# One kernel of attention, routed experts and a two-layer net: bias rows in another PSUM pool, added matmuls, earlier loads, other engines for two copies

## The chip, the core and the metric

The kernel runs on one core of a Trainium2 chip. The core has five engines with a queue each: TensorE (PE, its weight loads PEld), VectorE (DVE), ScalarE (ACT), GpSimd (POOL) and SyncE (SP), which here issues nearly all DMAs. The metric is the device time of one execution in microseconds. Comparisons are between medians of runs.

## What is computed

Three blocks follow each other: attention with a bias that depends on positions, a mixture of eight experts with one expert for each token, and a two-layer net with a cosine.

```python
# q, k, v: 4 batches x 8 heads x 576 x 64
scores = q @ k.T / 8
x = log1p(abs(i - j)) / log1p(max(i, 1))            # 576 x 576
bias = relu(x * w1 + b1) @ w2                       # 32 hidden units, one column for each head
attn = softmax(scores + bias) @ v
x = attn, heads side by side                        # 2304 tokens x 512
e = argmax(x @ w_gate)
x = gate(x) * sigmoid(x @ w_output_gate) * (relu(x @ w1[e]) @ w2[e])
h = x @ w_in                                        # 2304 x 2048
out = (h * cos(h)) @ w_out                          # 2304 x 512
```

All products are made in full fp32 precision: each factor is split into a high and a low part, and three products of parts are added.

## The kernel before

**The bias rows** (`bias_table`). The 576 rows of the bias are made in 36 groups of 16, in the order of `ROWS`. For a group, VectorE and ScalarE make four hidden tiles (hhD, hhA), TensorE multiplies them by w2 into a PSUM tile of two banks (`ps`, three of them in a pool that lives for this stage alone), ScalarE copies that into an SBUF tile `ev` (five buffers), and SP writes it to the DRAM tensor Bd. After the copy of a group, `after` (L480 on) issues loads that read bias rows back, by the table `BIAS_LOAD`: the entry for each of five blocks of query rows is the place in `ROWS` behind which its loads are put. `after` also makes the splits of the first pair, and at the last two groups it loads the q and k (Rqk), the V and the gating table of what comes next. `first` loads the first pair at the start.

**Attention.** The 16 pairs (two heads, one batch) are walked through in five steps u each. In a step, TensorE makes the scores of two query tiles into `ps_s` (two PSUM tiles of two banks, each step uses both), VectorE adds the bias rows (Bp, Bq), takes the minimum mn and leaves s, ScalarE takes the exponentials e, TensorE transposes the e of the step before into Tp (pool `ps_t`, two banks), ScalarE and VectorE copy that to eT, and TensorE multiplies eT by V into pa. The V products of a pair's second half run in the first steps of the next pair. `split` makes high and low parts (HL) of the next pair's q and k on GpSimd. Every engine's queue is in order, and the code's order is the queue's.

**The two-layer net** (`moe2`). The 2304 tokens are six groups of 384. A unit is a group with one half of the hidden units, eight steps of 128; the first six units are half 0 of each group, the next six are half 1. In step s TensorE makes the first layer's tile ph of step s (12 matmuls of 384 columns) and the second layer's part of step s - 4 (9 matmuls of 512 columns, into three PSUM tiles py). Between them stand tk (ScalarE, L1313), three instructions of VectorE that reduce the argument (L1318 to L1320), sine and square (ScalarE), tg (VectorE, L1403), gh (ScalarE, L1409) and gl (GpSimd, L1410). Meanwhile VectorE converts weights from 64-bit to 32-bit numbers (f32a, raw, L701 to L710). At the end of a unit of half 0 the three py are copied to SBUF (o) with factor -2 and written to Y1: the first and third by ScalarE (L1438), the second by VectorE (L1440). The next group's tokens are loaded to xg (one buffer) and split into xh (`split_x`, ScalarE) and xl (`lower_x`, GpSimd), one of four parts in each of steps 1 to 4 and 2 to 5 of a unit. The load of the group after that is issued in a unit's last step.

Of the kernel before, what the change touches and what calls it, by code (L numbers as in the profile page):

```python
# [331 lines left out]
BIAS_ON = _share()  # L332


def bias_table(tc, h, Bd, first, after):


    nc = tc.nc
    NQ = S // 4
    with tc.tile_pool(name="p0", bufs=1) as c, \  # L340
         tc.tile_pool(name="p0h", bufs=10) as hp_, \
         tc.tile_pool(name="p0e", bufs=5) as ep, \
         tc.tile_pool(name="p0ps", bufs=3, space=PSUM) as pp:
        W = c.tile([128, S], F32, name="W")
        cc = c.tile([128, 34 + NQ + S // 16], F32, name="cc")
        near, far = slice(0, 336), slice(336, S)
        nc.sync.dma_start(out=W[:, near], in_=h["t_rel"][:, near])
        nc.scalar.dma_start(out=cc, in_=h["cc"])
        nc.sync.dma_start(out=W[:, far], in_=h["t_rel"][:, far])
        first()  # L350
        w1c, b1c, w2b, psi, rp8 = cc[:, 0:1], cc[:, 1:2], cc[:, 2:34], cc[:, 34:34 + NQ], cc[:, 34 + NQ:]
        bp = c.tile([128, NQ], F32, name="bp")
        nc.vector.tensor_scalar(out=bp, in0=psi, scalar1=b1c, scalar2=None, op0=ALU.mult)
        slope = lambda t: nc.vector.tensor_scalar(out=W[:, t], in0=W[:, t], scalar1=w1c, scalar2=None, op0=ALU.mult)
        slope(near)
        pss = {}

        def evac(G):
            back, ahead = reach(G)
            ev = ep.tile([128, S + 15], F32, name="ev")  # L360
            ps, zero = pss.pop(G)
            parts = [(ev[:, 0:back + ahead], ps[:, zero - back:zero + ahead])]
            if G in MIRROR:
                parts = [(ev[:, 0:back], ps[:, 1:back + 1][:, ::-1]), (ev[:, back:back + ahead], ps[:, 0:ahead])]
            for dst, src in parts:
                nc.scalar.activation(out=dst, in_=src, func=AF.Copy, scale=rp8[:, G:G + 1])
            nc.sync.dma_start(out=Bd[:, 16 * G:16 * G + 16, S - 1 - back:S - 1 + ahead].rearrange("h i j -> i h j"),
                              in_=ev[:, 0:back + ahead])
            after(G)

        for at, G in enumerate(ROWS):
            ps = pp.tile([128, 1024], F32, name="ps")
            back, ahead = reach(G)
            n = max(back + 1, ahead)
            hs = []
            for ct in range(4):
                m = 4 * G + ct
                e = BIAS_ON[m]
                hh = hp_.tile([128, S], F32, name="hh" + e, bufs=dict(D=11, A=5)[e])
                hs.append(hh)  # L380
                if e == "A":
                    nc.scalar.activation(out=hh[:, 0:n], in_=W[:, 0:n], func=AF.Relu, bias=bp[:, m:m + 1], scale=1.0)
                else:
                    nc.vector.tensor_scalar(out=hh[:, 0:n], in0=W[:, 0:n], scalar1=bp[:, m:m + 1], scalar2=0.0,
                                            op0=ALU.add, op1=ALU.max)
            zero = 512 if max(back, ahead) <= 512 else back
            cuts = sorted({zero - back, zero, 512, zero + ahead})
            if G in MIRROR:
                zero, cuts = 0, [0, n]
            pss[G] = ps, zero  # L390
            for c0, c1 in zip(cuts, cuts[1:]):
                for ct in range(4):
                    x = hs[ct][:, c0 - zero:c1 - zero] if c0 >= zero else hs[ct][:, zero - c1 + 1:zero - c0 + 1][:, ::-1]
                    nc.tensor.matmul(ps[32 * ct:32 * ct + 32, c0:c1], w2b, x, start=True, stop=True)
            if at == 2:
                slope(far)
            if at >= 2:
                evac(ROWS[at - 2])
        evac(ROWS[-2])
        evac(ROWS[-1])  # L400


def attention(tc, h, ident, dram, xT, bpool, ps_t, gate, later, dense):
# [3 lines left out]
    with ExitStack() as ctx:  # L407
# [70 lines left out]
        def after(G):  # L478
            at = ROWS.index(G)
            for qt, when in enumerate(BIAS_LOAD):  # L480
                if at == when:
                    for i in range(NTL):
                        if TILES[i][0] == qt:
                            load_bias(0, i)
            if at == len(ROWS) - 3:
                for step in (0, 2, 1, 3):
                    split(0, step, nc.vector)
                split(0, 4)
            if at == len(ROWS) - 2:
                load(1)  # L490
            if at == len(ROWS) - 1:
                load_v(1)
                gate.fetch()

        def first():
            load(0)
            load_v(0)

        bias_table(tc, h, Bd, first, after)
        sp, ep = pool("p1s", 3, **rw), pool("p1e", 1, **rw)  # L500
        ps_s, ps_a = pool("ps_s", 2, space=PSUM, **rw), pool("ps_a", 1, space=PSUM)
        gate.pa = [ps_a.tile([128, 512], F32, name=f"pa{g}") for g in range(2)]
        ET = []
        for g in range(2):
# [3 lines left out]
        def scores(n, u):  # L508

            d = st[n]  # L510
            HL = d["HL"]
            ps = [ps_s.tile([128, 2, 512], F32, name="ps_s") for _ in of_unit(u)]
            for hf in range(2):
                sl = slice(hf * HF, (hf + 1) * HF)
                for x, (q, k) in enumerate(((0, 0), (1, 0), (0, 1))):
                    for par, p in enumerate(ps):
# [4 lines left out]
                            w, y = d["QR"][:, q, :], HL[:, 1, k, sl]  # L521
                        nc.tensor.matmul(p[:, hf, :HF], w, y, start=(x == 0), stop=(x == 2))  # L522
            d["ps"] = ps

        def softmax(n, u):
            d = st[n]
# [137 lines left out]
        gate.pa = None  # L664


BIAS_LOAD = (27, 31, 35, 35, 35)
BIAS_AT = (1, 2, 4)
AV_AT = {1: ((0, 0, 2), (0, 1, 2), (0, 2, 3), (0, 3, 3)),
         4: ((0, 4, 1), (1, 0, 1), (1, 1, 1), (1, 2, 2), (1, 3, 2), (1, 4, 2))}  # L670
# [661 lines left out]
def moe2(tc, h, dram, dense, later, wi, wo, bias, cv):  # L1332
# [4 lines left out]
    with ExitStack() as ctx:  # L1337
# [29 lines left out]
        def split_x(g, c):  # L1367
            if c == 0:
                xsp[g] = dense.x_tiles()
            nc.scalar.activation(out=xsp[g][0][:, c, :], in_=xg[g][:, c, :], func=AF.Copy)  # L1370
# [52 lines left out]
        def layer2(s):  # L1423
# [6 lines left out]
            for t in range(GT // 128):  # L1430
# [3 lines left out]
                if j == HC - 1:  # L1434
                    o = op.tile([128, DM], F32, name="o")
                    if half == 0:
                        if t % 2 == 0:
                            nc.scalar.activation(out=o, in_=acc[t], func=AF.Copy, scale=-2.0)  # L1438
                        else:
                            nc.vector.tensor_scalar(out=o, in0=acc[t], scalar1=-2.0, scalar2=None, op0=ALU.mult)  # L1440
                        nc.sync.dma_start(out=dram["Y1"][rows(g, t), :], in_=o)
                        continue
                    final = s == len(units) * HC - 1 and t == GT // 128 - 1
# [15 lines left out]
        for s in range(N + LAG3):  # L1459
# [11 lines left out]
            if s < N:  # L1471
                k, j = divmod(s, HC)
                if s == 0:
                    load_x(groups[1])
                nx = groups[k + 1]
                if nx != groups[k]:
                    if 1 <= j < 5:
                        split_x(nx, j - 1)
                    if 2 <= j < 6:
                        lower_x(nx, j - 2)  # L1480
                if j == HC - 1 and groups[k + 2] != groups[k + 1]:
                    load_x(groups[k + 2])
            if 0 <= s - LAG3 < N:
# [2 lines left out]
                    load_y(g)  # L1486


CONVERT2_AT = 4
MAGIC = 12582912.0  # L1490
INV2PI = 0.15915494309189535
PI2A = 6.28125
# [59 lines left out]
```

## Time and profile before

| | |
|---|---|
| median of 3 runs | 962.22 us (959.72 to 963.46) |
| the profiled execution | 960.94 us, its span 959.1 us |
| TensorE busy | 917.5 us (96%), weight loads 782.3 us |
| VectorE busy | 712.0 us (74%) |
| ScalarE busy | 549.9 us (57%) |
| GpSimd busy | 305.7 us (32%) |
| mean granted TensorE clock | 0.983 of 2.4 GHz |

The stages, in us from the start of the span: bias rows to about 47, attention to about 300, experts to about 535, the two-layer net to the end. The shares are means over all of them. The granted clock is 1.0 (2.4 GHz) or 0.5 (1.2 GHz) in any stretch, and the mean tells how much of the span lay at the lower level. A busy TensorE is one with matmuls under way; at the lower level each of them takes longer, so its busy share doesn't tell its pace.

### The profile page before, as it was taken

Reading aid. Unit: us, or ns where it says so; the run is one execution under the profiler, and the core shown is the slowest. Engines: PE = TensorE matmul, PEld = TensorE weight load, DVE = VectorE, ACT = ScalarE, POOL = GpSimd, SP = SyncE. Lnnn points to the kernel's source line nnn. Section 1 sums busy time; section 2 is a strip of 40 time slices with the busy share of each in tenths; the row PEclk is TensorE's granted clock in tenths of the full one; section 3 lists DMA queues with packets and bytes.
Section 4 is the critical chain, followed back from the end, with each engine's and each line's share of the span. In section 5 each row is a group of like instructions: output and inputs, shape, how many; then the busy total and the mean of one; then the engine's idle time right before and its main releaser. Section 6 shows DMA issues by size and latency. Waiting matters only on the chain.

```text
span 959.1 us, 19242 instructions
## 1 busy us (share of the span) xinstructions
PE 917.5 (96%) x7145; PEld 782.3 (82%) x7146; DVE 712.0 (74%) x1538; ACT 549.9 (57%) x1157; POOL 305.7 (32%) x394
## 2 busy tenths in 40 slices
PE   7989999999998999999899899999999999999996
PEld 4576666666666999999799789888888899999995
DVE  8956666667777577877795699999999966655652
ACT  8967777777776343353344555555555655555442
POOL 0034344444444022213330044334332433433421
PEclk9979999999999999999999999999999999999999
DMA  7973333523445665548774323443333413211121
GB/s 220 286 249 103 102 134 108 175 65 104 144 155 184 194 204 172 164 122 253 247 243 164 115 83 105 132 143 105 123 102 121 130 58 99 99 53 47 66 67 37
DMA packets 70066, 131.42 MB, mean 137 GB/s; under 512 B 7320, under 2 KB 24748, under 8 KB 69964
## 3 DMA queue, kind: packets, MB, share of 16 engines
q1 hardware_dynamic: 69532, 129.82, 42.2%
q8 instruction: 58, 0.95, 0.4%
q14 instruction: 44, 0.36, 0.1%
q10 hardware_dynamic: 432, 0.29, 0.1%
HBM read 91.76 MB, written 38.32 MB: 136 GB/s over the span
## 4 chain that ended last, share of the span: by engine, by line
PE 51%; DVE 17%; issue 5%; DMA 3%; ACT 1%; SPq 0%; POOL 0%; DVEq 0%; POOLq 0%; ACTq 0%
PE py L1433 12%; PE ph L1384 11%; PE pl L844 9%; PE po L862 8%; PE pa L600 4%; PE ps_s L522 3%; DVE tr L1319 2%; DVE tg L1403 2%; DVE tr L1320 2%; DVE f32a L701 2%; PE Tp L558 2%; DVE raw L708 1%; DVE f32a L703 1%; DVE raw L706 1%; DVE tk L1318 1%
## 5 line engine op out<-in xcount | busy, mean ns | idle before, releaser
L1410 POOL TENSOR_TENSOR gl<-tg,gh 128x384 fp32r<-128x384 f32 x96 | 98.6, 1027 | 253.7 <-ACT gh L1409 179.1
L532 DVE CUSTOM_DVE_ANT_0 s<-ps_s,Bp 128x576 f32<-128x576 f32 x112 | 81.0, 756 | 70.0 <-PE ps_s L522 58.4
L1384 PE MATMUL ph<-xh,w0h 128*128 128x384 f32 x384 | 130.4, 339 | 0.0
L1384 PE MATMUL ph<-xh,w0l 128*128 128x384 f32 x384 | 130.3, 339 | 0.0
L1384 PE MATMUL ph<-xl,w0h 128*128 128x384 f32 x384 | 130.1, 339 | 0.0
L1433 PE MATMUL py<-w1h,gh 128*128 128x512 f32 x288 | 114.7, 398 | 8.1 <-ACT gh L1409 4.5
L1433 PE MATMUL py<-w1h,gl 128*128 128x512 f32 x288 | 114.4, 397 | 0.0
L1433 PE MATMUL py<-w1l,gh 128*128 128x512 f32 x288 | 113.9, 395 | 0.0
L543 ACT ACTIVATE e<-s,mn 128x576 f32<-128x576 f32 x144 | 110.0, 766 | 3.6 <-DVE mn L532 2.6
L1313 ACT ACTIVATE tk<-ph,magic 128x384 f32<-128x384 f32 x96 | 55.1, 574 | 79.3 <-PE ph L1384 78.8
L1320 DVE SCALAR_TENSOR_TENSOR tr<-tk,tr 128x384 f32<-128x384 f32 x96 | 89.6, 933 | 3.3
L1318 DVE TENSOR_SCALAR tk<-tk 128x384 f32<-128x384 f32 x96 | 37.3, 389 | 63.4 <-ACT tk L1313 63.3
L847 ACT ACTIVATE hh<-pl 128x288 fp32r<-128x288 f32 x64 | 26.3, 410 | 100.7 <-PE pl L844 88.1
L522 PEld LDWEIGHTS ps_s<-HL 64*128 64x128 f32 x768 | 58.0, 191 | 30.2 <-DVE eT L571 12.3
L1409 ACT ACTIVATE gh<-tg 128x384 fp32r<-128x384 f32 x96 | 49.7, 518 | 54.3 <-DVE tg L1403 54.0
L844 PE MATMUL pl<-xh,w0h 128*128 128x288 f32 x256 | 78.3, 306 | 2.5 <-DVE hl L848 2.5
L522 PE MATMUL ps_s<-HL 64*128 64x288 f32 x768 | 77.2, 319 | 3.1 <-DVE mn L532 2.3
L844 PE MATMUL pl<-xl,w0h 128*128 128x288 f32 x256 | 76.3, 299 | 2.3 <-DVE xl L816 2.3
L1384 PEld LDWEIGHTS ph<-xh,w0h 128*128 128x128 f32 x384 | 72.8, 190 | 4.0
L1384 PEld LDWEIGHTS ph<-xl,w0h 128*128 128x128 f32 x384 | 72.5, 189 | 3.9
L844 PE MATMUL pl<-xh,w0l 128*128 128x288 f32 x256 | 75.6, 296 | 0.0
L862 PE MATMUL po<-hh,w1h 128*128 128x288 f32 x256 | 75.6, 295 | 0.0
(228 smaller groups left out, 2282.2 us busy)
## 6 DMA issues: line engine op xcount, KB each, us to landing
Bp<-in_w SPq DMA_DIRECT2D x38, 512.0 KB, 5.2
Bd<-ev SPq DMA_DIRECT2D x36, 295.5 KB, 3.8
Rqk<-in_qk SPq DMA_DIRECT2D x16, 576.0 KB, 4.0
raw<-in_w_in SPq DMA_DIRECT2D x32, 256.0 KB, 3.2
raw<-in_w_out SPq DMA_DIRECT2D x32, 256.0 KB, 3.2
Bp<-Bd SPq DMA_DIRECT2D x28, 288.0 KB, 4.3
X<-xT SPq DMA_DIRECT2D x7, 1152.0 KB, 5.1
xg<-X SPq DMA_DIRECT2D x10, 768.0 KB, 5.2
```

What stands on the lines that cost most here:

```text
L522: nc.tensor.matmul(p[:, hf, :HF], w, y, start=(x == 0), stop=(x == 2))
L532: nc.vector.tensor_tensor_reduce(out=h2(s), in0=ps[:, :, :HF], in1=h2(bias(hp, i)), scale=-0.125, scalar=3e38, op0=ALU.add, op1=ALU.min, a ...
L543: nc.scalar.activation(out=e[:, par, :], in_=s, func=AF.Exp, bias=mn, scale=-1.0, accum_out=acc)
L844: nc.tensor.matmul(ps[:, :HF], w[:, c, :], x[:, c, :], start=(n == 0), stop=(n == len(terms) - 1))
L862: nc.tensor.matmul(self.acc[d][:, :HF], w[:, ds_], x, start=(f == 0 and n == 0), stop=(f == self.FC - 1 and n == 2))
L1313: nc.scalar.activation(out=k, in_=hh, func=AF.Identity, scale=INV2PI, bias=magic)
L1318: nc.vector.tensor_scalar(out=k, in0=k, scalar1=-MAGIC, scalar2=None, op0=ALU.add)
L1320: nc.vector.scalar_tensor_tensor(out=r, in0=k, scalar=-PI2B, in1=r, op0=ALU.mult, op1=ALU.add)
L1384: nc.tensor.matmul(ps[:, :GT], w[:, c, :], x[:, c, :], start=(n == 0), stop=(n == 3 * NP_ - 1))
L1409: nc.scalar.activation(out=hi, in_=g, func=AF.Copy)
L1410: nc.gpsimd.tensor_tensor(out=lo, in0=g, in1=hi.bitcast(F32), op=ALU.subtract)
L1433: nc.tensor.matmul(acc[t], x[:, ts_], w, start=(j == 0 and n == 0), stop=(j == HC - 1 and n == 2))
```

## The change

- The PSUM tiles of the bias rows come from attention's own pool `ps_s` (two of each three groups) and from a pool `ps_b` with one tile (the third). `ps_a`, which took banks of its own, takes those of `ps_b` when the bias rows are done. `ev` has eight buffers in place of five.
- All loads of the first two pairs and of the gating table are issued by `first`, at the kernel's start. `BIAS_LOAD` puts the loads of the first three blocks of bias rows behind groups 25, 29 and 32 in place of 27, 31 and 35.
- In the first three steps of the first pair, `FILL` adds 12, 6 and 4 matmuls into the PSUM tiles Tp, whose results nobody reads.
- The three copies o at the end of a unit of half 0 are all ScalarE's.
- In the first unit alone, the next group is split in steps 3 to 6 (high) and 4 to 7 (low); in the others in the steps as before.

```diff
@@ bias_table(tc, h, Bd, bank, first, after)
-         tc.tile_pool(name="p0e", bufs=5) as ep, \
-         tc.tile_pool(name="p0ps", bufs=3, space=PSUM) as pp:
+         tc.tile_pool(name="p0e", bufs=8) as ep:
...
         for at, G in enumerate(ROWS):
-            ps = pp.tile([128, 1024], F32, name="ps")
+            ps = bank(at)
@@ attention, after
                 split(0, 4)
-            if at == len(ROWS) - 2:
-                load(1)
-            if at == len(ROWS) - 1:
-                load_v(1)
-                gate.fetch()
 
         def first():
-            load(0)
-            load_v(0)
-
-        bias_table(tc, h, Bd, first, after)
+            for n in range(2):
+                load(n)
+                load_v(n)
+            gate.fetch()
+
+        ps_s = pool("ps_s", 2, space=PSUM, **rw)
+        pair_s = lambda: ps_s.tile([128, 1024], F32, name="ps_s")
+        with tc.tile_pool(name="ps_b", bufs=1, space=PSUM) as ps_b:
+            bias_table(tc, h, Bd, lambda at: ps_b.tile([128, 1024], F32, name="ps_b") if at % 3 == 2 else pair_s(),
+                       first, after)
         sp, ep = pool("p1s", 3, **rw), pool("p1e", 1, **rw)
-        ps_s, ps_a = pool("ps_s", 2, space=PSUM, **rw), pool("ps_a", 1, space=PSUM)
+        ps_a = pool("ps_a", 1, space=PSUM, **rw)
@@ attention, scores
-            ps = [ps_s.tile([128, 2, 512], F32, name="ps_s") for _ in of_unit(u)]
+            ps = [h2(pair_s()) for _ in of_unit(u)]
...
             d["ps"] = ps
+            if n == 0 and u in FILL:
+                spare = [ps_t.tile([128, 512], F32, name="Tp") for _ in range(2)]
+                for i in range(FILL[u]):
+                    for par in range(2):
+                        r = slice(64 * par, 64 * par + 64)
+                        nc.tensor.matmul(spare[par][:, :HF], HL[r, 0, 0, 0:128], HL[r, 1, 0, 0:HF], start=True, stop=True)
...
-BIAS_LOAD = (27, 31, 35, 35, 35)
+BIAS_LOAD = (25, 29, 32, 35, 35)
+FILL = {0: 6, 1: 3, 2: 2}
@@ moe2, layer2
                     if half == 0:
-                        if t % 2 == 0:
-                            nc.scalar.activation(out=o, in_=acc[t], func=AF.Copy, scale=-2.0)
-                        else:
-                            nc.vector.tensor_scalar(out=o, in0=acc[t], scalar1=-2.0, scalar2=None, op0=ALU.mult)
+                        nc.scalar.activation(out=o, in_=acc[t], func=AF.Copy, scale=-2.0)
@@ moe2, the loop over steps
-                    if 1 <= j < 5:
-                        split_x(nx, j - 1)
-                    if 2 <= j < 6:
-                        lower_x(nx, j - 2)
+                    if 0 <= j - FIRST_AT[k > 0] < 4:
+                        split_x(nx, j - FIRST_AT[k > 0])
+                    if 0 <= j - FIRST_AT[k > 0] - 1 < 4:
+                        lower_x(nx, j - FIRST_AT[k > 0] - 1)
...
-CONVERT2_AT = 4
+CONVERT2_AT, FIRST_AT = 4, (3, 1)
```

How this stands in the queues, at three places. Lines are those of each kernel; a row is a line, an operation, out<-in and the size of what is written.

TensorE, from the last matmul of the bias rows into the first pair, before and after (ps_s are scores, Tp transposes or the added matmuls):

```order
L394 MATMUL ps<-hhD,cc 32x16
L522 MATMUL ps_s<-HL 128x288 x24
L558 MATMUL Tp<-ident,e 128x64 x16
L522 MATMUL ps_s<-HL 128x288 x12
L558 MATMUL Tp<-ident,e 128x64 x16
L522 MATMUL ps_s<-HL 128x288 x12
```

```order
L393 MATMUL ps_b<-hhD,cc 32x16
L522 MATMUL ps_s<-HL 128x288 x12
L529 MATMUL Tp<-HL 128x288 x12
L522 MATMUL ps_s<-HL 128x288 x12
L529 MATMUL Tp<-HL 128x288 x6
L564 MATMUL Tp<-ident,e 128x64 x16
L522 MATMUL ps_s<-HL 128x288 x12
L529 MATMUL Tp<-HL 128x288 x4
L564 MATMUL Tp<-ident,e 128x64 x16
```

The added matmuls stand behind the scores of a step and ahead of the transposes of the step before.

SP, the DMAs from the kernel's start to the first pair's steps (Bd<-ev are row writes, Bp and Bq bias rows read back):

```order
L451 DMA Rqk<-in_qk 128x1152
L456 DMA V<-in_v 128x640
L367 DMA Bd<-ev 16x8x591 x28
L442 DMA Bp<-Bd 128x576 x2
L367 DMA Bd<-ev 16x8x591 x4
L442 DMA Bp<-Bd 128x576 x2
L367 DMA Bd<-ev 16x8x591 x3
L451 DMA Rqk<-in_qk 128x1152
L367 DMA Bd<-ev 16x8x591
L442 DMA Bp<-Bd 128x576 x3
L442 DMA Bq<-Bd 128x576
L445 DMA Bq<-Bd 64x576 x2
```

```order
L164 DMA g<-in_gc 128x160
L366 DMA Bd<-ev 16x8x591 x26
L441 DMA Bp<-Bd 128x576 x2
L366 DMA Bd<-ev 16x8x591 x4
L441 DMA Bp<-Bd 128x576 x2
L366 DMA Bd<-ev 16x8x591 x3
L441 DMA Bp<-Bd 128x576 x2
L366 DMA Bd<-ev 16x8x591 x3
L441 DMA Bp<-Bd 128x576
L441 DMA Bq<-Bd 128x576
L444 DMA Bq<-Bd 64x576 x2
```

The loads of q, k, V and g stand ahead of all row writes now, and three blocks of bias rows ahead of the last three writes.

ScalarE, the start of the two-layer net:

```order
L1313 ACTIVATE tk<-ph,magic 128x384
L1370 ACTIVATE xh<-xg 128x384
L1313 ACTIVATE tk<-ph,magic 128x384
L1398 ACTIVATE tr<-tr 128x384
L1399 ACTIVATE tr<-tr 128x384
L1370 ACTIVATE xh<-xg 128x384
```

```order
L1320 ACTIVATE tk<-ph,magic 128x384 x2
L1405 ACTIVATE tr<-tr 128x384
L1406 ACTIVATE tr<-tr 128x384
L1320 ACTIVATE tk<-ph,magic 128x384
L1405 ACTIVATE tr<-tr 128x384
L1406 ACTIVATE tr<-tr 128x384
L1416 ACTIVATE gh<-tg 128x384
L1377 ACTIVATE xh<-xg 128x384
```

The first xh stood behind one tk; it now stands behind the first gh.

## Rows read from the trace of the kernel before

**Rows 1.** Windows: stretch, us, busy us (instructions) of PE PEld DVE ACT POOL, clock, DMA, GB/s.

```profile
2.00:10.00 8.00, 5.35 (x40) 3.53 (x41) 6.39 (x22) 4.84 (x11) 0.38 (x2) 1.00 0.68 200
10.00:40.00 30.00, 29.72 (x422) 17.13 (x420) 30.00 (x85) 29.59 (x52) 0.00 (x0) 1.00 0.88 265
...
50.20:63.80 13.60, 11.87 (x108) 10.47 (x109) 7.19 (x19) 7.82 (x20) 4.20 (x8) 0.50 0.85 290
...
548.50:555.30 6.80, 5.09 (x12) 3.70 (x13) 6.58 (x12) 5.51 (x12) 4.58 (x4) 0.50 0.00 0
...
623.60:627.00 3.40, 3.40 (x11) 3.01 (x10) 3.26 (x6) 2.27 (x5) 2.28 (x2) 0.50 0.41 154
...
584.00:762.00 178.00, 174.40 (x859) 155.62 (x857) 170.44 (x309) 102.28 (x198) 60.72 (x56) 0.99 0.37 115
```

**Rows 2.** Timeline of VectorE's score readings: start us, us, instruction [idle before <-what ended it].

```profile
49.03 0.76 DVE L532 CUSTOM_DVE_ANT_0 s<-ps_s,Bp 128x576 f32<-128x576 f32 x1 [1.09 <-PE ps_s L522]
...
56.78 0.76 DVE L532 CUSTOM_DVE_ANT_0 s<-ps_s,Bp 128x576 f32<-128x576 f32 x1 [2.59 <-DMA Bp<-Bd]
...
66.51 0.76 DVE L532 CUSTOM_DVE_ANT_0 s<-ps_s,Bp 128x576 f32<-128x576 f32 x1 [2.02 <-PE ps_s L522]
...
69.10 0.76 DVE L532 CUSTOM_DVE_ANT_0 s<-ps_s,Bp 128x576 f32<-128x576 f32 x1 [0.56 <-PE ps_s L522]
...
75.62 0.76 DVE L532 CUSTOM_DVE_ANT_0 s<-ps_s,Bp 128x576 f32<-128x576 f32 x1 [1.21 <-PE ps_s L522]
...
81.38 0.76 DVE L532 CUSTOM_DVE_ANT_0 s<-ps_s,Bp 128x576 f32<-128x576 f32 x1 [1.99 <-PE ps_s L522]
```

**Rows 3.** Timeline: first scores on TensorE, and SP's issues in the first pair.

```profile
48.07 1.05 PE L522 MATMUL ps_s<-HL 64*128 64x288 f32 x11 [0.61 <-ACT ev L366]
...
49.90 2.71 SPq L442 DMA_DIRECT2D Bp<-Bd  x3
...
56.00 1.14 SPq L445 DMA_DIRECT2D Bq<-Bd  x2
```

**Rows 4.** DMA issues of 0 to 70 us: count, size, median us to landing.

```profile
Bp<-Bd SPq DMA_DIRECT2D x9, 288.0 KB, 5.6
...
Bq<-Bd SPq DMA_DIRECT2D x2, 144.0 KB, 4.0
```

**Rows 5.** Timelines at the start of the two-layer net: ScalarE, TensorE, VectorE.

```profile
545.60 0.52 ACT L1370 ACTIVATE xh<-xg 128x384 fp32r<-128x384 f32 x1 [6.29 <-DMA xg<-X]
...
550.17 0.80 PE L1433 MATMUL py<-w1h,gh 128*128 128x512 f32 x1 [4.47 <-ACT gh L1409]
...
551.02 0.57 DVE L1318 TENSOR_SCALAR tk<-tk 128x384 f32<-128x384 f32 x1
```

**Rows 6.** Chain that ended last: start us, us, piece; and the window of line L1384 alone.

```profile
578.25 2.10 PE py L1433 x9
580.35 2.11 PE ph L1384 x12
...
582.45:763.62 181.17, 94.00 (x494) 88.78 (x494) 0.99 0.37 116
```

**Rows 7.** Waits: TensorE in 553 to 706 and 706 to 765, ScalarE in 553 to 762.

```profile
PE py L1433 <- DVE o L1440: 2.8, 3, 2.0
...
PE py L1433 <- DVE o L1440: 0.8, 2, 0.7
...
ACT xh L1370 <- DMA xg<-X: 4.8, 3, 2.5
```

**Rows 8.** Groups in 545 to 800: VectorE's copies o; busy us, ns of one, idle.

```profile
L1440 DVE TENSOR_SCALAR o<-py 128x512 f32<-128x512 f32 x6 | 4.1, 685 | 0.1
```

**Rows 9.** Timeline: TensorE behind the second copy; GpSimd and TensorE at 705.

```profile
622.97 0.51 PE L1433 MATMUL py<-w1h,gh 128*128 128x512 f32 x1 [1.96 <-DVE o L1440]
...
704.62 1.02 POOL L1410 TENSOR_TENSOR gl<-tg,gh 128x384 fp32r<-128x384 f32 x1 [2.84 <-ACT gh L1409]
...
705.70 0.50 PE L1433 MATMUL py<-w1h,gl 128*128 128x512 f32 x1
```

More of the change, by code (lines that the diff above doesn't have):

```diff
@@ L332, with bias_table @@
 BIAS_ON = _share()
-def bias_table(tc, h, Bd, first, after):
+def bias_table(tc, h, Bd, bank, first, after):
     nc = tc.nc
```

## The prediction

> **What bounds the kernel now.** I read the windows by stage first, because a mean over the span hides that three stages have three limits. In the stage of the bias rows (10 to 40 us) VectorE is busy 30.00 of 30 us, ScalarE 29.59, and the DMA engines 0.88 of the time [rows 1]; that stage is VectorE's, and nothing in the change shortens it. Then I looked for stretches at the granted clock 0.5 (TensorE at 1.2 GHz): 50.2 to 63.8, where attention begins, and 548.5 to 555.3, where the two-layer net (`moe2`) begins; a third, 3.4 us long, stands at 623.6 [rows 1]. Third, what ended the idle time in front of them, in order of time. At 545 TensorE stands 4.47 us for ScalarE's gh, and ScalarE itself stood 6.29 us for the load of xg [rows 5]. After that TensorE runs nine second-layer matmuls, 2.10, and twelve first-layer ones, 2.11, in turn: 4.2 us a step [rows 6]. Up to 762 VectorE is busy 170.44 of 178 us [rows 1], yet what TensorE waits for there is mostly one instruction, VectorE's copy o of a finished result, five times, 3.6 us [rows 7]. So both engines are near their limit, and each part of the change has to be asked which of them it helps.
>
> **Part 1, attention's first pair.** One pair is five steps, and each step's first reading of scores by VectorE marks it: 49.03 for the first pair, 66.51 for the second, 81.38 for the third [rows 2]. The first pair takes 17.48 us, the second 14.87. The second has no disturbance: first step 2.59 (66.51 to 69.10), next two 6.52, last two 5.76. The middle two carry the products with V of the pair before, which the first pair doesn't have. I therefore give the first pair 3 x 2.59 + 5.76 = 13.5 us, a gain of 4.0; the upper bound of its time is the second pair's 14.87, a gain of 2.6. This needs three things.
> The clock has to stay at 1.0. In 50.2 to 63.8 TensorE's rows show 11.87 busy us of 13.6, but at 0.5, where every matmul lasts longer. The 22 added matmuls (12, 6 and 4) have the shape of the scores, 11 of which take 1.05 us at the full clock [rows 3]. The twelve stand between the first scores, done at about 49.1, and the second, which wait for both of VectorE's readings, about 50.5 (two times 0.76 behind 49.03 [rows 2]): 1.1 us of work in a gap of 1.4, so they delay nothing. The six and four stand ahead of transposes that wait for ScalarE or for the copies out of the same PSUM tiles anyhow: also nothing. Should the clock fall all the same, the twelve take twice as long, and the first pair goes at the rate that its last three steps had, 9.73 from 56.78 to 66.51, so 16.2 us for five: gain 1.3, which comes from the DMA wait alone.
> The bias rows have to be there. VectorE waited 2.59 us for them in the third step [rows 2]; they were issued from 49.90 on [rows 3], behind the load of the next pair's q and k, 128 x 1152 numbers or 576 KB. Now the rows of the third step go out ahead of the last three row writes, and the load stands at the start of the kernel; even at 5.6 us to landing [rows 4] they are there at about 52 and are wanted at 53.9. The fifth step's rows are late next: they wait for the last row write, went out at 56.00 and take 4.0 us [rows 3, 4], so 60.0, and would be wanted at 58.6. The load that is gone from in front of them is 576 KB at the stretch's 290 GB/s [rows 1], 2.0 us, so 58.0: just in time. If not, up to 1.4 is lost.
> The start itself: the second tile of scores waited 0.61 us for ScalarE's last copy [rows 3], since the new PSUM pool lay on the old one's banks; now it waits for the copy before. The low halves of q and k end about as late, so I take 0.3, between 0 and 0.6.
> Sum of part 1: **4.2**, between 1.3 and 4.6.
> The early inputs (a second pair's 896 KB and a table of 80 KB, ahead of all row writes on SP's queue) go out in the first 10 us, when 2 to 10 shows the DMA engines 0.68 busy at 200 GB/s against 265 behind it [rows 1], and the writes have eight buffers in place of five. Cost taken: 0. If that cover is gone, 976 KB at 265 GB/s [rows 1], 3.8 us, pushes the row writes.
>
> **Part 2, start of the two-layer net.** ScalarE's queue is in order: the first conversion xh of the next group stood as its second instruction and held it until the load landed at 545.6 [rows 5]. Now seven more instructions, gh of step 0 the last of them, stand ahead of it. VectorE can then work through two whole steps before 545.6; the instruction that starts the fourth tile's reduction began at 551.02 [rows 5] and can begin one ScalarE tk after the conversion, at about 546.6: VectorE's chain is 4.4 us earlier. TensorE alone would gain more: its 4.47 us of idle time and half of the 5.09 us of work that it did at clock 0.5 [rows 1], 7.0 in all. What is late next: the last low half xl of the next group, on GpSimd two steps later than before, behind gl; by my reckoning the ninth first-layer tile may stand about 1 us for it, inside what TensorE is ahead of VectorE there. The load of the group after that waits for it too.
>
> **Part 3, the copies.** Six copies of 0.685 us leave VectorE, 4.1 us [rows 8], and join ScalarE, which is busy 102.28 of 178 us [rows 1] and stands there anyhow between its two others: at about the same length, beside other work. TensorE's own side: 2.8 + 0.8 us of waits [rows 7], the longest (1.96 us [rows 9]) followed by the 3.4 us at clock 0.5, of which half, 1.7, is lost: 5.3. The count says the same from the other end: in the 181.17 us from 582.45 lie 494 first-layer matmuls [rows 6], 41 tiles of twelve, and with them 42 second-layer tiles; at 2.11 and 2.10 that is 174.7 us, 6.5 less.
>
> **The sum of parts 2 and 3** is not 7.0 + 5.3, since VectorE follows at 96%. GpSimd's gl of one step ran from 704.62 to 705.64, and the matmul that reads it started at 705.70 [rows 9]: there VectorE's chain had no lead left. Up to that place TensorE can gain only what VectorE's chain gains: 4.4 and four copies of 0.685, 7.1. Behind it, two more copies stop delaying TensorE, 0.8 [rows 7]. Sum **7.9**; upper bound 7.0 + 6.5 = 13.5, if VectorE's instructions get shorter where they stand differently; lower bound 5.4, if the 1 us for xl comes off the front (3.4) and half of the copies' 4.1 goes into waits for ScalarE.
> 4.2 + 7.9 = 12.1. The profiled execution took 960.94 us, 959.1 of it span; it would take 948.8. It lies 1.3 under the median of 962.22, and the median after is **950.1**.
>
> **The rivals.**
> A, TensorE sets the pace all through the net: 4.2 + 13.5, 944.5. For it: it waited for gl hardly at all outside of 705. Against: VectorE's 170.44 of 178.
> B, the clock falls in the first pair although it is filled: 1.3 in place of 4.2, 953.0. For it: the rows tell the state, not what would have held it.
> C, the group split is not out of the way: ScalarE stands at the new place as long as at the old, two steps later, and only the copies count, by their time on VectorE: 4.2 + 4.1, 953.9. This is the case that the change doesn't do what it says. Against: gh of the first two steps no longer depends on the load.
> D, the early inputs cost 3.8 us in the bias stage: 953.9. The rows show the DMA engines 0.68 busy at 2 to 10 and 0.88 behind it [rows 1]. The Trainium skill, "DMA: Bandwidth & Descriptors", section "Issuing engines are not separate DMA queues", says that all transfers run on the same 16 engines and interleave; by that rule the early loads and the row writes share them, and 3.8 is what it would cost; the trace shows both loads in one stage, and no row on how they share it.
> E, slower: the load of xg comes through at every group. ScalarE waited three times for it in later groups, 4.8 us, 2.5 at most [rows 7], and VectorE's lead hid it. With the lead spent, each of five group changes could stop TensorE for 1.6 us and cost a fall of the clock (1.7): 16.5 against 12.1, 966.6. It decides from the point at which xg lands later than two steps, 8.4 us, behind its issue, since VectorE then has nothing left to work on. Against: the waits move with VectorE's chain, which ScalarE follows.
>
> **How the numbers follow.** Forecast 0.63 (its own range, with the bounds above, 947 to 955.5); A 0.11, B 0.12, C 0.06, D 0.04, E 0.04. Range 944 to 956: it leaves out E, and some of A, C and D. A measurement tells from no change what is over 0.5%, 4.8 us: under 957.4 is faster. All but E and the worst of C and D together lie there: faster 0.92, same 0.05, slower 0.03.
>
> **What would show it.** Right: granted clock 1.0 from 45 to 70; the third step without a DMA wait; the second pair's first reading at about 62; ScalarE's gh ahead of its first xh and no 4.5 us of idle TensorE; no wait for o. Wrong: clock 0.5 at 50 (B); VectorE with the same 170 us but TensorE still waiting, now for ScalarE's o or xl (C, E); ScalarE waiting for row writes at 10 to 45 (D). If TensorE waits for gl nowhere, A is right and the sum of parts 2 and 3 too small.

## The result and the profile after

The changed kernel takes 952.75 us (950.41 to 953.99) against 962.88 for the kernel before, a ratio of 0.9895 with an interval of 0.9872 to 0.9918: 10.1 us faster, where 12.1 were forecast and 944 to 956 was the range. Run once more, beside a later group of kernels, it took 952.27 against 963.76 (0.9881, 0.9863 to 0.9899). The profiled execution took 950.41 us with a span of 948.7, 10.4 under the span of before.

Where the 10.4 us lie is read from three marks: the first score reading of the third pair, the first matmul of the two-layer net, and the end. First VectorE's score readings, as in [rows 2]: start us, us, instruction, idle time before it and what ended it.

```profile
48.87 0.76 DVE L538 CUSTOM_DVE_ANT_0 s<-ps_s,Bp 128x576 f32<-128x576 f32 x1 [0.89 <-PE ps_s L522]
...
53.91 0.76 DVE L538 CUSTOM_DVE_ANT_0 s<-ps_s,Bp 128x576 f32<-128x576 f32 x1 [0.52 <-PE ps_s L522]
...
59.89 0.76 DVE L538 CUSTOM_DVE_ANT_0 s<-ps_s,Bq 128x576 f32<-128x576 f32 x1 [1.28 <-DMA Bq<-Bd]
...
63.25 0.76 DVE L538 CUSTOM_DVE_ANT_0 s<-ps_s,Bp 128x576 f32<-128x576 f32 x1 [1.98 <-PE ps_s L522]
...
78.12 0.76 DVE L538 CUSTOM_DVE_ANT_0 s<-ps_s,Bp 128x576 f32<-128x576 f32 x1 [1.98 <-PE ps_s L522]
```

The first pair takes 14.38 us (63.25 - 48.87) where it took 17.48, the third step no longer waits for a DMA, and the third pair begins 3.26 us earlier than before (81.38 - 78.12).

The net begins with this matmul, in the trace of before and in that of the changed kernel:

```profile
535.10 0.34 PE L1384 MATMUL ph<-xh,w0h 128*128 128x384 f32 x1
```

```profile
533.00 0.34 PE L1391 MATMUL ph<-xh,w0h 128*128 128x384 f32 x1
```

Only 2.10 of the 3.26 us are left there. The net itself then takes 424.0 us before (959.1 - 535.1) and 415.7 after: 8.3 us, for which 7.9 were forecast. Windows of the changed kernel (columns as in [rows 1]): the bias rows, the first pair, two stretches in the experts' stage, and the stretch of the net that answers to 584 to 762 before.

```profile
10.00:40.00 30.00, 29.72 (x423) 17.32 (x420) 30.00 (x84) 29.80 (x52) 0.00 (x0) 1.00 0.88 263
50.20:63.80 13.60, 11.97 (x153) 9.24 (x155) 8.24 (x21) 9.82 (x24) 6.11 (x12) 1.00 0.76 246
304.06:307.47 3.41, 3.41 (x18) 2.75 (x17) 3.03 (x14) 1.62 (x3) 0.00 (x0) 0.50 0.03 7
457.65:461.06 3.41, 3.41 (x17) 3.41 (x16) 2.47 (x6) 0.41 (x1) 0.74 (x1) 0.50 0.78 244
...
574.00:752.00 178.00, 176.69 (x871) 156.25 (x870) 171.46 (x311) 105.83 (x206) 63.30 (x58) 1.00 0.37 117
```

The granted clock is 1.0 in the first pair, and in the net it is 0.5 only from 942.35 on, behind the last matmul (940.3). In the experts' stage there are two stretches at 0.5: the one at 304.06 answers to one at 306.16 before, and the one at 457.65 the kernel before didn't have. In the net's window TensorE is busy 176.69 of 178 us, 2.3 more than before, and VectorE 171.46, 1.0 more.

The start of the net, ScalarE and then TensorE, which answers to [rows 5]; then the waits of TensorE in 540 to 760 (engine, line, waited for: us in total, times, longest), which answer to [rows 7]:

```profile
541.25 0.51 ACT L1416 ACTIVATE gh<-tg 128x384 fp32r<-128x384 f32 x1
543.59 0.53 ACT L1377 ACTIVATE xh<-xg 128x384 fp32r<-128x384 f32 x1 [1.83 <-DMA xg<-X]
...
543.42 0.40 PE L1440 MATMUL py<-w1h,gh 128*128 128x512 f32 x1
```

```profile
PE ph L1391 <- POOL xl L1381: 1.5, 1, 1.5
PE py L1440 <- POOL gl L1417: 1.1, 3, 0.4
PE py L1440 <- ACT gh L1416: 0.2, 1, 0.2
```

ScalarE's first gh stands ahead of its first xh, TensorE's first second-layer matmul follows without idle time, and the waits for o are gone. In their place stand one wait for xl and short ones for gl and gh.

### The profile page after: what moved, and what is told of

It reads as the page before. It is cut to its first block, busy times and chain, and to the rows that moved or that the text cites. A ratio compares the mean times of both kernels' runs of the same rounds, so it can differ in the third digit from the quotient of the medians.

```text
span 948.7 us, 19290 instructions
## 1 busy us (share of the span) xinstructions
PE 914.4 (96%) x7167; PEld 778.2 (82%) x7168; DVE 708.7 (75%) x1532; ACT 551.7 (58%) x1163; POOL 306.2 (32%) x394
## 4 chain that ended last, share of the span: by engine, by line
PE 56%; issue 10%; POOL 6%; DMA 3%; DVE 3%; SPq 1%; ACT 1%; POOLq 0%; DVEq 0%
PE py L1440 14%; PE ph L1391 14%; PE pl L851 10%; PE po L869 10%; POOL gl L1417 3%; PE pa L606 3%; PE ps_s L522 2%; POOL xl L1381 2%; PE Tp L564 1%; DMA Wo<-f32a 1%; DMA xc<-in_w 1%; DMA xg<-X 1%; DVE f32a L708 1%; DMA Cd<-cr 1%; SPq L210 0%
## 5 line engine op out<-in xcount | busy, mean ns | idle before, releaser
L1327 DVE SCALAR_TENSOR_TENSOR tr<-tk,tr 128x384 f32<-128x384 f32 x96 | 90.1, 939 | 3.3
L522 PEld LDWEIGHTS ps_s<-HL 64*128 64x128 f32 x768 | 55.8, 185 | 27.6 <-DVE eT L577 11.8
L869 PE MATMUL po<-hl,w1h 128*128 128x288 f32 x256 | 75.9, 296 | 0.0
L869 PE MATMUL po<-hh,w1l 128*128 128x288 f32 x256 | 75.8, 296 | 0.0
```

Source lines behind the costliest of these rows:

```text
L869: nc.tensor.matmul(self.acc[d][:, :HF], w[:, ds_], x, start=(f == 0 and n == 0), stop=(f == self.FC - 1 and n == 2))
L1327: nc.vector.scalar_tensor_tensor(out=r, in0=k, scalar=-PI2B, in1=r, op0=ALU.mult, op1=ALU.add)
```

## The experiments

All times are medians, each against runs of the kernel before on the same chip. The last column is read from one trace of each kernel: the time from the first first-layer matmul to the end of the span. The net as changed stands in six of these kernels and takes 414.7 to 416.5 there, and the net as before stands in two and takes 424.0 and 425.7; so a difference of 2 us in this column is not yet one between kernels.

| kernel | us | ratio to before (95%) | net, us |
|---|---|---|---|
| before | 962.5 to 963.8 | 1 | 424.0 |
| changed | 952.75 | 0.9895 (0.9872 to 0.9918) | 415.7 |
| changed, again | 952.27 | 0.9881 (0.9863 to 0.9899) | 414.8 |
| no added matmuls | 951.57 | 0.9891 (0.9868 to 0.9914) | 414.7 |
| net as before | 959.61 | 0.9972 (0.9954 to 0.9990) | 425.7 |
| copies as before | 955.47 | 0.9936 (0.9912 to 0.9959) | 418.4 |
| split as before | 955.22 | 0.9935 (0.9911 to 0.9959) | 420.1 |
| bias and input loads as before, added matmuls in | 952.69 | 0.9887 (0.9865 to 0.9909) | 414.8 |
| the same, no added matmuls | 953.98 | 0.9904 (0.9884 to 0.9924) | 416.5 |
| input loads as before | 954.17 | 0.9898 (0.9877 to 0.9920) | 416.1 |
| low parts a step earlier | 951.87 | 0.9885 (0.9865 to 0.9905) | 417.0 |
| subtraction on ScalarE | 946.63 | 0.9830 (0.9814 to 0.9846) | 410.7 |
| both | 945.82 | 0.9814 (0.9798 to 0.9830) | 411.0 |
| both, copies as before | 946.92 | 0.9834 (0.9817 to 0.9851) | 411.3 |

### Are the added matmuls what holds the clock?

```diff
-FILL = {0: 6, 1: 3, 2: 2}
+FILL = {}
```

> The changed kernel without the 22 added matmuls, all else as changed. Theory (they hold the clock): the granted clock falls to 0.5 at about 50 and stays there for most of the first pair, and the pair goes at the rate of the last three steps of the kernel before: 2 to 3 us slower than the changed kernel, 955 to 956. Rival 1 (the clock fell because the third step stood for bias rows, and these are early now): clock 1.0 from 45 to 70 all the same, time that of the changed kernel, 952.8. Rival 2 (the added matmuls stand in the way of scores): faster by up to 1.1 us. In the trace the second pair's first score reading decides: 63.3 (rival 1), 65 to 66 (theory), below 63 (rival 2).

951.57 us, no slower than with them. Score readings and window of this kernel's first pair:

```profile
48.93 0.76 DVE L538 CUSTOM_DVE_ANT_0 s<-ps_s,Bp 128x576 f32<-128x576 f32 x1 [0.88 <-PE ps_s L522]
...
62.67 0.76 DVE L538 CUSTOM_DVE_ANT_0 s<-ps_s,Bp 128x576 f32<-128x576 f32 x1 [1.89 <-PE ps_s L522]
```

```profile
50.20:63.80 13.60, 11.69 (x148) 8.93 (x148) 8.84 (x23) 10.39 (x26) 6.09 (x12) 1.00 0.74 250
```

The clock stays at 1.0, as rival 1 of this run says: with the loads early, the pair needs no filling. But the second pair begins at 62.67, 0.6 earlier than with the added matmuls, and under 63 was the mark of rival 2: they do stand in the way, though of the transposes and not of scores. With them the six of the second step go first on TensorE, and ScalarE waits longer for the transposes behind them (with them, TensorE and ScalarE; then ScalarE without them):

```profile
51.14 0.68 PE L529 MATMUL Tp<-HL 64*128 64x288 f32 x6
...
52.57 0.60 ACT L575 ACTIVATE eT<-Tp 128x512 f32<-128x512 f32 x1 [1.19 <-PE Tp L564]
```

```profile
51.99 0.60 ACT L575 ACTIVATE eT<-Tp 128x512 f32<-128x512 f32 x1 [0.55 <-PE Tp L564]
```

From there ScalarE needs 2.66 us for each step in both kernels (this copy begins at 52.57, 55.23, 57.88 and 60.54 with them, at 51.99, 54.65, 57.31 and 59.97 without), so the 0.6 is still there at the pair's end. The ratios are too coarse to show it (0.9891 against 0.9895 and 0.9881). The next three runs take the early loads away.

```diff
+            if at == len(ROWS) - 2:
+                load(1)
+            if at == len(ROWS) - 1:
+                load_v(1)
+                gate.fetch()
...
-            for n in range(2):
-                load(n)
-                load_v(n)
-            gate.fetch()
+            load(0)
+            load_v(0)
...
-BIAS_LOAD = (25, 29, 32, 35, 35)
+BIAS_LOAD = (27, 31, 35, 35, 35)
```

> The changed kernel with the bias rows' loads, and the second pair's loads, at their old places, but with the 22 added matmuls. Theory 1 (the matmuls hold the clock): the third step waits 2.6 us for bias rows as in the kernel before, yet the granted clock is 1.0 from 50 to 64 and the pair takes about 16 us: 1.5 to 2 us over the changed kernel, 954.6. Theory 2 (only the early rows held the clock, since the kernel without the 22 matmuls held it too): the clock falls all the same, the pair takes 17.2 us: 3 us over, 955.7.

The same with `FILL = {}`:

> As the run before, without the 22 added matmuls: of part 1 only the PSUM tiles are left. Theory 1 and theory 2 alike: clock 0.5 from about 50 to 60 or longer, pair as before (17.2 us), 955.7 to 956. By theory 1 this is 1.1 to 1.5 us over the run before, by theory 2 it is the same. If part 1 is worth less than the 2.9 us that it showed by itself, under 955.

And with only the loads of the second pair and the gating table back:

> The changed kernel with the second pair's loads and the gating table at their old places, at the end of the bias rows; bias rows early, 22 matmuls in. Theory (the fifth step's rows are what is late next): 576 KB go ahead of them, so the fifth step waits 2 us longer, 3.3 instead of 1.28, and the second pair's first reading is at 65.2: 2 us over the changed kernel, 954.8. Rival D (the early loads cost time in the stage of the bias rows): the first reading moves from 48.9 to under 48, and the time is that of the changed kernel or less, 951 to 952.8.

The changed kernel ran beside them:

> The changed kernel once more, beside the runs of this group, so that they stand against it on the same chip: 952.8, between 950.5 and 954. Theory on the clock fall in the experts' stage at 458 (it hangs on when the 2 us wait for hl falls, not on the change): in some executions there, in others not. Rival: it comes with the change, and stands in this profile too.

With late bias rows and the added matmuls, the window of the first pair, and then the readings of its third step and of the second pair's first:

```profile
50.20:63.80 13.60, 9.70 (x115) 8.18 (x115) 7.13 (x19) 7.70 (x19) 3.73 (x8) 0.87 0.88 290
```

```profile
57.32 0.76 DVE L541 CUSTOM_DVE_ANT_0 s<-ps_s,Bp 128x576 f32<-128x576 f32 x1 [3.85 <-DMA Bp<-Bd]
...
66.71 0.76 DVE L541 CUSTOM_DVE_ANT_0 s<-ps_s,Bp 128x576 f32<-128x576 f32 x1 [1.98 <-PE ps_s L525]
```

The same two views without the added matmuls:

```profile
50.20:63.80 13.60, 10.92 (x106) 9.49 (x105) 7.23 (x19) 7.80 (x19) 4.00 (x8) 0.65 0.88 299
```

```profile
56.95 0.76 DVE L541 CUSTOM_DVE_ANT_0 s<-ps_s,Bp 128x576 f32<-128x576 f32 x1 [2.91 <-DMA Bp<-Bd]
...
66.93 0.76 DVE L541 CUSTOM_DVE_ANT_0 s<-ps_s,Bp 128x576 f32<-128x576 f32 x1 [2.24 <-PE ps_s L525]
```

With late rows the added matmuls do lift the clock (mean 0.87 against 0.65), and yet the second pair begins at 66.7 and 66.9, as in the kernel before (66.51 [rows 2]). The rows of the third step land at about 57 in all three, and that decides: at the full clock VectorE only waits longer for them (3.85 us against 2.91, and 2.59 before). Theory 1 is right about the clock in part (it falls once, at 58.99, for 3.4 us) and wrong about the pair, which takes 17.76 us (66.71 - 48.95) where it said about 16.

With only the input loads late, the fourth step waits for bias rows, and the second pair begins at 66.12:

```profile
57.95 0.76 DVE L541 CUSTOM_DVE_ANT_0 s<-ps_s,Bp 128x576 f32<-128x576 f32 x1 [1.81 <-DMA Bp<-Bd]
...
66.12 0.76 DVE L541 CUSTOM_DVE_ANT_0 s<-ps_s,Bp 128x576 f32<-128x576 f32 x1 [3.68 <-PE ps_s L525]
```

The clock is 0.5 from 58.5 to 65.4 there, though the added matmuls are in the steps before. So early places for the bias rows' loads are not enough by themselves; the rows come in time when the input loads are out of their way too. No run put the bias rows' loads alone back. The first reading stood at 49.03 here and at 48.87 and 48.96 with the input loads early, so these cost the bias stage nothing, and rival D falls.

In the traces the second pair begins 2.8 to 3.7 us later in these three runs than in the two of the changed kernel (63.25 and 63.34). The medians (952.69, 953.98, 954.17) are only 0.4 to 1.9 us above 952.27, with overlapping intervals, and the first two lie under what was expected of them, the second under its mark of 955 for a part 1 that is worth less than 2.9. Executions of one kernel lie up to 5.6 us apart here (951.06 to 956.67), so the times don't tell these kernels apart. For part 1 as a whole they say 2.7 us, between 1.0 and 4.4, by the next run.

### What is each part worth?

> The changed kernel with the two-layer net as before (VectorE copies the second result, all groups split in steps 1 to 4): part 1 alone. Theory: part 1 is worth 2.1 to 3.5 us by the profiles (3.5 through attention, 2.1 left where the net begins), so 959.4 to 960.8, and parts 2 and 3 are worth 7 to 8.5. Rival (the parts help each other, the early start of attention being worth nothing by itself): 962.9. Rival (all of 4.2 arrives): 958.7.

959.61: part 1 alone is worth 2.9 us between the medians, inside what was expected. Then one part of the net at a time.

```diff
-                        nc.scalar.activation(out=o, in_=acc[t], func=AF.Copy, scale=-2.0)
+                        if t % 2 == 0:
+                            nc.scalar.activation(out=o, in_=acc[t], func=AF.Copy, scale=-2.0)
+                        else:
+                            nc.vector.tensor_scalar(out=o, in0=acc[t], scalar1=-2.0, scalar2=None, op0=ALU.mult)
```

> The changed kernel with the second copy of a finished result on VectorE again: parts 1 and 2 without part 3. Theory (VectorE's chain sets the pace up to 705): four copies of 0.685 and 0.8 us of waits behind that, 3.5 us slower than the changed kernel, 956.3. Rival A (TensorE's own waits count): 5.3 slower, 958.1. Rival (with the early split there is lead enough, the copies are hidden): 952.8.

```diff
-CONVERT2_AT, FIRST_AT = 4, (3, 1)
+CONVERT2_AT, FIRST_AT = 4, (1, 1)
```

> The changed kernel with the first group split in steps 1 to 4 as before: parts 1 and 3 without part 2. Theory (VectorE's chain): 4.4 us slower than the changed kernel, 957.2, and TensorE stands 4.5 us for gh at about 543 with a fall of the clock behind it. Rival A (TensorE's idle time and clock count): 7.0 slower, 959.8. Rival C (ScalarE stands as long at either place): 952.8.

TensorE's waits in 530 to 790, with the copies as before and then with the split as before:

```profile
PE py L1440 <- DVE o L1447: 4.4, 5, 2.5
PE ph L1391 <- POOL xl L1381: 0.7, 1, 0.7
```

```profile
PE py L1440 <- ACT gh L1416: 3.9, 1, 3.9
PE py L1440 <- POOL gl L1417: 1.1, 3, 0.4
```

Each part brings its own wait back. The ratios, the first three on one chip: neither 0.9972, split alone 0.9936, copies alone 0.9935, both 0.9881 and 0.9895 in two measurements. In us of 962.5 the split alone is worth 3.5, the copies alone 3.6, both 7.4 to 8.8: they add, within the intervals of some 2 us.

Taken from the changed kernel the copies were expected to cost 3.5 by VectorE's chain and 5.3 by TensorE alone, the split 4.4 and 7.0. In the traces they cost 1.9 to 3.7 (418.4 less 416.5 to 414.7) and 3.6 to 5.4 (420.1 less the same): the chain's numbers lie inside, TensorE's outside. By the ratios they cost 3.9 to 5.3 and 3.9 to 5.2, which speaks against 7.0 for the split and doesn't decide for the copies.

### Does VectorE's chain set the pace behind that?

If it does, making the front of TensorE's queue earlier brings nothing, and taking work out of the chain brings what is left.

```diff
-                    if 0 <= j - FIRST_AT[k > 0] - 1 < 4:
-                        lower_x(nx, j - FIRST_AT[k > 0] - 1)
+                    low = j - FIRST_AT[k > 0] - (k > 0)
+                    if 0 <= low < 4:
+                        lower_x(nx, low)
```

> The changed kernel with the first group's low parts in steps 3 to 6 instead of 4 to 7, the same steps as its high parts. Theory: the wait of the ninth first-layer tile for xl (1.0 and 1.5 us in two profiles, with 1.2 to 1.8 lost there) goes, and what VectorE's chain lost by it stays lost up to 705: between 0 and 1.5 us faster than the changed kernel's 952.3, 951.5. Rival (VectorE's chain sets the pace anyway): waits for gl grow by as much, 952.3.

```diff
             turns(nc, k, d[s]["h"], bias)
+            nc.scalar.activation(out=k, in_=k, func=AF.Copy, bias=-MAGIC)
...
-            reduce(nc, r, d[s]["k"], d[s]["h"])
+            k, hh = d[s]["k"], d[s]["h"]
+            nc.vector.scalar_tensor_tensor(out=r, in0=k, scalar=-PI2A, in1=hh, op0=ALU.mult, op1=ALU.add)
+            nc.vector.scalar_tensor_tensor(out=r, in0=k, scalar=-PI2B, in1=r, op0=ALU.mult, op1=ALU.add)
```

> The changed kernel with the subtraction of the magic number (VectorE's 0.36 to 0.39 us in each of 96 steps) as a second instruction of ScalarE behind tk. Theory (VectorE's chain is what still holds TensorE up to 705): the 3.9 us that the second-layer steps 17 to 36 of the changed kernel take beyond 4.21 each go, 948.4. Rival 1 (ScalarE, one more 0.5 us instruction in a step and a longer chain to gh): waits for gh appear, 952 to 955. Rival 2 (what holds it is the copies' place on ScalarE): 952.3.

> Both edits of the two runs before. Theory: their gains add, since with VectorE relieved the front of TensorE's queue counts at once: 5.4 us, 946.9, and TensorE's steps are 4.2 us from the second one to the end. Rival (they overlap): no better than the better of the two, 948.4.

> The run before with the second copy of a finished result on VectorE again, as in the kernel before. Theory (the copies cost by filling VectorE's chain, which now has 15 us of room): at most 0.5 us over the run before, 947.4. Rival (they cost because TensorE stands for an instruction that waits in VectorE's queue, however full that is over the stretch): 2 to 3.3 us over it, 949 to 950.2, with waits for VectorE's o as in the kernel before.

TensorE's waits in 530 to 790, first with the low parts earlier, then with the subtraction on ScalarE, then with both and the copies as before:

```profile
PE py L1440 <- POOL gl L1417: 1.8, 5, 0.4
PE py L1440 <- ACT gh L1416: 0.2, 1, 0.2
```

```profile
PE ph L1391 <- POOL xl L1381: 0.3, 1, 0.3
```

```profile
PE py L1443 <- DVE o L1450: 0.8, 1, 0.8
```

Low parts earlier: the wait for xl (1.5 and 1.0 us) is gone, those for gl grew from 1.1 to 1.8, and the time is the same (951.87). That speaks for the rival of this run, by which the chain takes the gain back, but it doesn't settle it: up to 1.5 us was at stake, and the interval is wider than that. In this one trace the net takes 417.0, no less than in the six kernels with the changed net.

Subtraction on ScalarE, the window that answers to the last one above:

```profile
574.00:752.00 178.00, 178.00 (x891) 160.52 (x890) 162.41 (x274) 129.74 (x259) 75.78 (x61) 1.00 0.41 128
```

No wait for gl or gh is left, TensorE is busy in the whole of it, and the time is 946.63, 5.6 to 6.1 under the two medians of the changed kernel (4.9 to 6.3 by the ratios), where 3.9 were expected. This kernel's net takes 410.7 us, 13.3 less than before: the 13.5 that TensorE alone could gain (7.0 + 6.5 in the prediction) are there once VectorE's chain has room. Both edits together, 945.82, are the fastest kernel here, but its interval overlaps that of the subtraction alone and its net takes 411.0 against 410.7, so no gain on top is shown. With room in the chain, the copies on VectorE cost 1.1 us between the medians, with overlapping intervals, 0.3 in the net (411.3 against 411.0), and one wait of 0.8 in place of five of 4.4 in total. That lies between the 0.5 of the theory and the 2 to 3.3 of its rival. The trace is on the theory's side, by which most of what the copies cost comes from how full VectorE is; the times alone don't show it.

## Why the prediction was right, step by step

**Part 1: 4.2 forecast, 3.26 in the trace and 2.7 by the times.** The term that was wrong in kind is the cost of the added matmuls. The prediction took it as nothing, because the six and four "stand ahead of transposes that wait for ScalarE or for the copies out of the same PSUM tiles anyhow". They did not wait: without the six the transposes began at 51.20, with them at 51.85, ScalarE fell back by 0.6 us, and the second pair begins at 62.67 without and at 63.25 and 63.34 with them. That is 0.6 of the 0.9 that are missing; most of the rest is the size of the pair itself, 13.74 us without them (62.67 - 48.93) where 13.5 were taken. Both show in the last two steps, for which I took the second pair's 5.76 us: 6.74 here (63.25 - 56.51), 6.04 without the added matmuls (62.67 - 56.63). TensorE's timeline of the changed kernel there:

```profile
56.63 0.46 PE L564 MATMUL Tp<-ident,e 64*128 64x64 f32 x8 [0.16 <-ACT e L549]
57.39 0.46 PE L564 MATMUL Tp<-ident,e 64*128 64x64 f32 x8 [0.30 <-ACT e L549]
...
59.29 0.46 PE L564 MATMUL Tp<-ident,e 64*128 64x64 f32 x8 [0.45 <-ACT e L549]
60.05 0.47 PE L564 MATMUL Tp<-ident,e 64*128 64x64 f32 x8 [0.30 <-ACT e L549]
```

The transposes stand 1.21 us for ScalarE's exponentials, and 0.25 without the added matmuls. In the second pair the products with V of the pair before have put TensorE behind ScalarE by then, and it doesn't stand for them. The fifth step's rows were late too, by 1.28 us at VectorE, as the prediction allowed. But in the second execution of the changed kernel, with no such wait, the second pair began at 63.34, so the rows cost nothing here. The steps on the third step's rows (wanted at 53.9, read at 53.91 without a DMA wait), on the start (0.3 forecast, 49.03 - 48.87 = 0.16) and on the early loads (0) were right. That the clock would hold was right, but not for the reason that the text leaned on: it held without the added matmuls, and with late rows it fell in spite of them.

**Between the two places** the prediction let the gain pass through untouched. In this execution 1.2 us of it went in the experts' stage: there the lead over the kernel before is 3.13 us at 444.78 (the matmul that began at 447.91 before) and 1.95 at 466.91 (468.86). TensorE waits 2.1 us for hl at 456.88, where it waited 2.5 before, but here the clock fell behind it (457.65). The second execution of the changed kernel has no fall there and none at 304:

```profile
304.06:307.47 3.41, 3.08 (x26) 2.54 (x25) 3.29 (x15) 2.06 (x4) 0.00 (x0) 1.00 0.02 5
457.65:461.06 3.41, 3.41 (x31) 2.06 (x29) 3.25 (x8) 0.41 (x1) 0.74 (x1) 1.00 0.82 247
```

Its net began at 531.96, 3.1 us earlier than before, and it took 948.54 us. So such falls come and go between executions of one kernel. What one costs is not shown more closely: from the second pair's first reading to the net the traces of all kernels take 468.5 to 469.7 us with no fall in the experts' stage (three) and 469.3 to 471.9 with two (four).

**Parts 2 and 3: 7.9 forecast, 8.3 measured (7.5 to 11 over all traces with either net), by the mechanism that was named.** VectorE's fourth reduction was to begin 4.4 us earlier than 551.02; it began at 544.62, which is 4.3 within the net (6.4, less 2.1 for the earlier start):

```profile
544.62 0.36 DVE L1325 TENSOR_SCALAR tk<-tk 128x384 f32<-128x384 f32 x1 [2.01 <-ACT tk L1320]
```

The place without lead came earlier by the forecast amount. This is the matmul of the changed kernel that answers to the one at 705.70 in [rows 9]:

```profile
696.71 0.50 PE L1440 MATMUL py<-w1h,gl 128*128 128x512 f32 x1 [0.36 <-POOL gl L1417]
```

It comes 8.99 us earlier (705.70 - 696.71), 6.9 of it within the net; 7.1 was the sum of 4.4 and four copies. Behind it came 1.4 (10.4 - 8.99) where 0.8 was forecast. The wait for xl that "may stand about 1 us" was 1.48 here and 1.0 in the second execution:

```profile
561.55 0.45 PE L1391 MATMUL ph<-xl,w0h 128*128 128x384 f32 x1 [1.48 <-POOL xl L1381]
```

So of the 12.1 forecast, 0.9 were lost in the first pair, 1.2 in the experts' stage, and 0.4 came on top in the net, which leaves the 10.4 of the traces. The 1.2 came by chance in this execution, and misses of different sign made the sum look better than its terms.

**The rivals.** A fell by the waits for gl, and the run with the subtraction on ScalarE shows why: it is what the net does when VectorE isn't in the way. B fell, the clock held. C fell: ScalarE waits 1.83 us for xg at the new place in place of 6.29. D fell by the first reading. E: ScalarE waited four times for xg, 6.6 us, 2.4 at most, and TensorE never for what hangs on it but the one xl. One bound of the prediction doesn't follow from its own terms: the lower end of "947 to 955.5" should be 944.1 by the gains of 4.6 and 13.5 that it names, which is where rival A lies. The forecast itself doesn't use it.

## What to carry to other kernels

Where another engine follows with no lead left (VectorE here, busy 96%), a wait that is removed in front of TensorE was worth what that engine's chain gained, not what TensorE would gain by itself. The place at which the chain has no lead left gave that number, and work taken out of the chain gave the rest. Before filling an idle engine to hold its clock, look at what it idles for: here earlier loads removed the idle time and the fall with it, and the filling cost 0.6 us in the trace, because what is put ahead in a queue delays what stands behind it.

## What the runs showed of the hardware

The two-input instruction of VectorE that reads SBUF alone (L1327) takes 0.56 us or about 1.17 (in the changed kernel's net 38 of 96 under 0.57, the others 1.16 to 1.33), and its neighbour that reads a PSUM tile (L1326) always 0.55. Timelines of the changed kernel, VectorE and GpSimd:

```profile
545.60 0.56 DVE L1327 SCALAR_TENSOR_TENSOR tr<-tk,tr 128x384 f32<-128x384 f32 x1
...
549.14 0.55 DVE L1326 SCALAR_TENSOR_TENSOR tr<-tk,ph 128x384 f32<-128x384 f32 x1
549.72 1.17 DVE L1327 SCALAR_TENSOR_TENSOR tr<-tk,tr 128x384 f32<-128x384 f32 x1
...
549.47 1.01 POOL L1417 TENSOR_TENSOR gl<-tg,gh 128x384 fp32r<-128x384 f32 x1 [1.38 <-ACT gh L1416]
550.43 1.33 POOL L1381 TENSOR_TENSOR xl<-xg,xh 128x384 fp32r<-128x384 f32 x1
```

The long ones lie beside GpSimd's gl or xl, the short ones beside none or a rest of one. The Trainium skill, "GPSIMD Engine Reference", section "1. Specifications", says that GpSimd shares its SBUF interfaces with VectorE and that they contend where VectorE has two SBUF inputs or runs in a mode with two ports; the trace agrees on the two inputs, with 0.56 against 1.17. Groups in 584 to 740 (busy us, mean ns), changed kernel and then the one with the subtraction on ScalarE:

```profile
L1327 DVE SCALAR_TENSOR_TENSOR tr<-tk,tr 128x384 f32<-128x384 f32 x37 | 42.7, 1154 | 1.3
...
L708 DVE TENSOR_SCALAR f32a<-raw 128x256 int32<-128x256 int32 x24 | 11.7, 487 | 0.0
```

```profile
L708 DVE TENSOR_SCALAR f32a<-raw 128x256 int32<-128x256 int32 x26 | 22.2, 855 | 0.0
L1404 DVE SCALAR_TENSOR_TENSOR tr<-tk,tr 128x384 f32<-128x384 f32 x38 | 21.2, 558 | 1.3
```

Moving the subtraction also moved this collision, from L1327 (1154 to 558 ns; it is L1404 there) to the weight conversion behind it (L708, 487 to 855 ns). L708 reads one tile of SBUF and takes 0.28 us, or about 1.1 where GpSimd is at work beside it; no run shows in which mode it runs. How much of the gain of that run is the 0.36 us taken out of each step, and how much the collision or the shorter hand-over from one engine to the next, was not separated.
